# Two 2 MB stores taken out of SyncE's stream and issued as 64 GpSimd pieces and 4 SyncE pieces

## The chip, the cores and the metric

The kernel runs on one core of a Trainium2 chip. The metric is the time of one execution on the device in microseconds. Before the change the median of three runs is 730.11 us (729.95 to 731.11).

## The reference

One decode step of a transformer block, forward and backward. `x` is one token of width 640; the caches hold 32 heads of 8192 rows of 128 values, bf16; `d...` below are the gradients that the kernel must return as well.

```python
xn  = layernorm(x)
q   = (xn @ wq) as 32 heads of 128
p_h = softmax(k_cache_h @ q_h / sqrt(128))        # 8192 values per head
o_h = p_h @ v_cache_h
out = x + concat(o_h) @ wo + (silu(xn @ w1) * (xn @ w3)) @ w2
# backward from grad_out: dx, dk_cache, dv_cache, dwq, dwo, dw1, dw3, dw2
# dv_cache_h = outer(p_h, do_h)       dk_cache_h = outer(ds_h, q_h)
```

Each head reads a K and a V of 2 MB and writes a dK and a dV of 2 MB. That is nearly all of the traffic: 151 MB read and 151 MB written.

## The kernel before, in words

A K or V of one head is one tile `kv` of 128 partitions with 8192 values each (16 KB per partition); ten such slots exist. `head(h)` runs for h = 0 to 31: TensorE transposes the K and V tiles and multiplies them with q and do, ScalarE evicts, VectorE makes the softmax. One head later, VectorE overwrites the same tiles with the outer products (L466, two halves for V, two for K): `outers_a(h-1)` makes dV and calls `store("V", h-1)`, `outers_b(h-1)` finishes dK and calls `store("K", h-1)`. So V28, V29, V30 and V31 below are the tiles whose dV is stored, K28 to K31 those whose dK is stored.

What orders the work around the change:

- **SyncE's queue.** All K and V loads and stores go through `fifo` (L105) on SyncE, in program order: a store, then the next load as soon as slots allow. Each is one transfer of 128 rows of 16 KB. At the end stands this order: load K31, store K27, load V31, then store V28, K28, V29, K29, V30, K30, V31, K31, then a part of the last `wo` and `wq` gradients, then the two small output rows (L849, L867). SyncE issues in order, so a store that isn't ready holds back all that stand behind it. V31's load is the last load.
- **GpSimd's queue.** GpSimd carries the weight groups: one store of `wo_g` (640 KB, L507) and five of `wq_g` (128 KB each, L527) per group of four heads. In heads 29 to 31 these are the `wo_g` store of group 6 and its five `wq_g` stores. At the very end `store_group` (L505 to L511) splits the `wo_g` and `wq_g` stores of the last group by partitions: 0 to 67 by SyncE, 68 to 72 and 73 to 127 by GpSimd.
- **Eight semaphores per kind of queue.** Transfers of SyncE take eight completion semaphores in turn, those of GpSimd another eight. A transfer that takes a semaphore again waits until the transfer eight before it on that kind of queue has landed.

The lines that the change touches:

```python
    def store(kind, h):
        t = kv_tiles.pop((kind, h))
        if kind == "K":
            hd.pop(h)
        fifo((dkc if kind == "K" else dvc)[h], t[:])
        free_slots.append(t)
        load_next()
```

Of the kernel before, what the change touches and what calls it, by code (L numbers as in the profile page):

```python
# [21 lines left out]
def kernel(  # L22
# [22 lines left out]
    nc = tc.nc  # L45
    H = A_k_cache.shape[1]
# [10 lines left out]
    KVN = J * DH  # L57
# [18 lines left out]
    dkc = out_2.rearrange("b h (p j) d -> (b h) p (j d)", p=P)  # L76
    dvc = out_3.rearrange("b h (p j) d -> (b h) p (j d)", p=P)
# [26 lines left out]
    def fifo(out_, in_):  # L104
        nc.sync.dma_start(out_, in_)  # L105
# [16 lines left out]
    def load_next():  # L122
        if not pending or len(free_slots) < lag[0]:
            return
        kind, h = pending.pop(0)
        t = free_slots.pop(0)
        fifo(t[:], (kc if kind == "K" else vc)[h])
        kv_tiles[(kind, h)] = t
# [335 lines left out]
    def outer(dst, vec, pair, lo, hi):  # L464
        n = hi - lo
        nc.vector.tensor_tensor(  # L466
            dst[:, lo * DH:hi * DH].rearrange("p (j a b) -> p j a b", a=DH // 2, b=2),
            vec.rearrange("p (a b) -> p a b", b=2).unsqueeze(1).to_broadcast([P, n, DH // 2, 2]),
            pair[:, lo:hi, :].unsqueeze(2).to_broadcast([P, n, DH // 2, 2]), ALU.mult)
# [4 lines left out]
    def outer_k(h, lo, hi):  # L474
        outer(kv_tiles[("K", h)], hd[h]["qd"][:, 0, :], hd[h]["U2"], lo, hi)

    def store(kind, h):
        t = kv_tiles.pop((kind, h))
        if kind == "K":
            hd.pop(h)  # L480
        fifo((dkc if kind == "K" else dvc)[h], t[:])
        free_slots.append(t)
        load_next()

# [248 lines left out]
    def outers_a(h):  # L733
        outer_v(h, 0, J // 2)
        outer_v(h, J // 2, J)
        store("V", h)
        outer_k(h, 0, J // 2)

    def outers_b(h):
        outer_k(h, J // 2, J)  # L740
        store("K", h)
# [156 lines left out]
```

## Time and profile before

| what | value |
|---|---|
| median of three runs | 730.11 us |
| the profiled execution | 730.34 us, of which the span on the core is 728.6 us |
| TensorE, VectorE, ScalarE, GpSimd busy | 84%, 63%, 52%, 6% of the span |
| DMA, mean over the span | 417 GB/s, 303.52 MB |
| SyncE's queue (q1 in the profile) | 277.09 MB |
| GpSimd's queue (q0 in the profile) | 25.61 MB |
| last load (V31) issued, landed | 659.79 us, 685.38 us |
| last outer product done, its store issued | 704.85 us, 704.87 us |
| last output row issued | 716.75 us |

Times inside the execution are counted from the start of the span. The profile page has the busy share of each engine, the share of the 16 DMA engines in 40 slices, and the DMA queues with packets and bytes. Other views of the trace list who waited for whom, the busy time in chosen stretches, and the DMA packets in a stretch. The trace also records each DMA packet with its start, its duration, its size and its queue (but not the engine that moved it), and each increment of a completion semaphore by a DMA engine; for a transfer of 128 rows there are 16 of these, one for each DMA engine. From these come the times at which the first and the last engine finished a transfer.

### The profile page before, as it was taken

How to read it: one execution, taken by the hardware profiler on the slowest of the kernel's cores; microseconds unless marked ns; L12 is line 12 of the kernel's file. 1: busy time of each engine (PE TensorE's matmuls, PEld its weight loads, DVE VectorE, ACT ScalarE, POOL GpSimd, SP SyncE). 2: the span in 40 equal slices, each digit the busy share in tenths (PEclk: the TensorE clock that was granted, in tenths of full speed). 3: DMA queues.
4: the chain of work that ended last, by engine and by line, in shares of the span. 5: the costliest groups of instructions: out<-in, count | busy, mean ns of one | idle time of the engine just before them, and what ended most of it. 6: DMA issues, size and time to landing. Idle time of an engine off the chain costs nothing.

```text
span 728.6 us, 12970 instructions
## 1 busy us (share of the span) xinstructions
PE 608.4 (84%) x5193; PEld 378.6 (52%) x5193; DVE 459.7 (63%) x811; ACT 376.6 (52%) x727; POOL 44.1 (6%) x75
## 2 busy tenths in 40 slices
PE   4989489999899989878897997978898889979840
PEld 2547366655565556544564554544555556545520
DVE  4169646688868776666466665646746657576482
ACT  3640736665666566554464554645555446555510
POOL 0010100010001000101000000001000000000000
PEclk9996799999999999998898998999999989998965
DMA  9999999999999999999999999999999999999994
GB/s 355 399 411 419 432 425 430 426 426 422 419 426 429 428 423 427 426 429 425 427 428 426 430 421 430 429 428 429 424 427 430 426 430 429 426 430 427 430 402 157
DMA packets 28186, 303.52 MB, mean 417 GB/s; under 512 B 3379, under 2 KB 5355, under 8 KB 11486
## 3 DMA queue, kind: packets, MB, share of 16 engines
q1 hardware_dynamic: 21962, 277.09, 89.8%
q0 software_dynamic: 6160, 25.61, 8.8%
q8 instruction: 41, 0.67, 0.4%
q14 instruction: 19, 0.16, 0.1%
q10 hardware_dynamic: 4, 0.00, 0.0%
HBM read 151.34 MB, written 151.34 MB: 415 GB/s over the span
## 4 chain that ended last, share of the span: by engine, by line
DMA 49%; PE 37%; DVE 7%; ACT 4%; issue 1%; SPq 0%; ACTq 0%; DVEq 0%
DMA out_dram<-kv 21%; PE pT L318 17%; DMA kv<-in_A_k_cache_dram 15%; DMA kv<-in_A_v_cache_dram 11%; PE sA L339 5%; PE dA L339 4%; PE X L433 4%; DVE kv L466 3%; PE m L356 2%; DMA wo_g<-in_A_wo_dram 2%; ACT KT L320 1%; ACT kv L642 1%; PE gu_ps L561 1%; DVE side L257 1%; PE dh_ps L572 1%
## 5 line engine op out<-in xcount | busy, mean ns | idle before, releaser
L320 ACT COPY KT<-pT 128x512 f32<-128x512 f32 x512 | 288.5, 588 | 229.3 <-PE pT L318 210.4
L318 PE MATMUL pT<-ident_f,kv 128*128 128x128 f32 x2048 | 307.9, 289 | 54.5 <-DMA kv<-in_A_k_cache_dram 40.7
L318 PEld LDWEIGHTS pT<-ident_f,kv 128*128 128x128 f32 x2048 | 236.8, 149 | 146.1 <-PE pT L318 51.9
L466 DVE TENSOR_TENSOR kv<-qd,U 128x4096 bf16<-128x4096 bf16 x64 | 146.1, 2285 | 0.0
L466 DVE TENSOR_TENSOR kv<-qd,P 128x4096 bf16<-128x4096 bf16 x64 | 143.6, 2285 | 0.0
L433 PE MATMUL X<-kv,Z 128*32 128x512 bf16 x1024 | 102.0, 431 | 1.8 <-DVE Z L450 1.8
L339 PE MATMUL dA<-KT,qz 128*32 128x512 bf16 x512 | 85.4, 413 | 0.0
L339 PE MATMUL sA<-KT,qz 128*32 128x512 bf16 x512 | 82.5, 402 | 0.0
L416 DVE SCALAR_TENSOR_TENSOR U<-m,P 128x64 bf16<-128x64 f32 x32 | 7.5, 233 | 105.7 <-PE m L356 105.7
L433 PEld LDWEIGHTS <-Z 128*32 128x32 bf16 x1024 | 33.9, 104 | 38.1 <-issue 13.2
L339 PEld LDWEIGHTS <-qz 128*32 128x32 bf16 x1024 | 29.5, 95 | 41.0 <-issue 38.5
L382 DVE TENSOR_REDUCE mrow<-m 128x1 f32<-128x64 f32 x32 | 7.2, 224 | 51.6 <-PE m L356 51.4
L356 PEld LDWEIGHTS m<-selc,KT 64*128 64x128 f32 x256 | 22.0, 147 | 31.8 <-ACT KT L346 18.0
L356 PE MATMUL m<-selc,KT 64*128 64x64 f32 x256 | 31.1, 246 | 8.0 <-ACT KT L346 8.0
L527 POOL DMA_DIRECT2D out_dram<-wq_g x35 | 19.1, 547 | 223.1 <-DVE wq_g L524 124.3
L376 ACT CAST qd<-pT 128x256 bf16<-128x256 f32 x32 | 11.9, 373 | 38.8 <-DVE kv L466 30.4
L389 DVE TENSOR_REDUCE negM<-m 128x1 f32<-128x128 f32 x32 | 9.3, 292 | 32.8 <-PE m L386 32.8
L522 DVE SCALAR_TENSOR_TENSOR wq_g<-wq_g,side 128x512 bf16<-128x512 bf16 x40 | 27.3, 683 | 0.0
L257 DVE SCALAR_TENSOR_TENSOR side<-wo_g,g_bc 128x640 bf16<-128x640 bf16 x32 | 26.3, 820 | 0.6 <-DMA wo_g<-in_A_wo_dram 0.2
L507 POOL DMA_DIRECT2D out_dram<-wo_g x7 | 5.3, 761 | 282.5 <-DVE qz L363 240.3
L448 DVE SCALAR_TENSOR_TENSOR U<-m,P 128x128 bf16<-128x128 f32 x32 | 11.4, 356 | 16.8 <-PE m L446 16.8
L346 ACT COPY KT<-dA 64x512 f32<-64x512 f32 x32 | 18.6, 582 | 5.1 <-PE dA L339 5.0
(163 smaller groups left out, 386.0 us busy)
## 6 DMA issues: line engine op xcount, KB each, us to landing
out_dram<-kv SPq DMA_DIRECT2D x64, 2048.0 KB, 30.7
kv<-in_A_k_cache_dram SPq DMA_DIRECT2D x32, 2048.0 KB, 17.2
kv<-in_A_v_cache_dram SPq DMA_DIRECT2D x32, 2048.0 KB
wq_g<-in_A_wq_dram POOLq DMA_DIRECT2D x7, 640.0 KB, 13.6
wo_g<-in_A_wo_dram POOLq DMA_DIRECT2D x7, 640.0 KB, 19.4
out_dram<-wo_g POOLq DMA_DIRECT2D x7, 640.0 KB, 11.3
out_dram<-wq_g POOLq DMA_DIRECT2D x35, 128.0 KB, 6.8
kv<-in_B_w_dram SPq DMA_DIRECT2D x2, 1728.0 KB
```

The source lines that it names most:

```text
L257: nc.vector.scalar_tensor_tensor(junk[:], G_["wo"][:, hh, :], 1.0, g_bc[:], ALU.mult, ALU.mult, accum_out=G_["do"][:, hh:hh + 1])
L318: nc.tensor.transpose(pT[:, k * P:(k + 1) * P], W3[:, 4 * c + k, :], ident_f[:])
L320: nc.scalar.copy(KT[:].rearrange("p k w -> p (k w)"), pT[:])
L339: nc.tensor.matmul(S_[kind][q:q + QW, :], lhsT=S_["qz"][:, o:o + QW], rhs=KTb[c][:, par, :], start=(c0 == 0 and par == 0), stop=(c0 == NCH ...
L346: nc.scalar.copy(XS[0:QH].rearrange("p k w -> p (k w)"), S_.pop(kind)[0:QH, :])
L356: nc.tensor.matmul(S_["m"][:, b0:b0 + 4 * J].rearrange("p (x c k t) -> p k x c t", x=4, k=4, t=2)[:, k], lhsT=XS[0:QH, k, :], rhs=selc[0:Q ...
L376: nc.scalar.copy(qd[:].rearrange("p a d -> p (a d)"), hd[h].pop("ps_r"))
L433: nc.tensor.matmul(xg["X"][q:q + QW, :], lhsT=Z[:, o:o + QW], rhs=W[:, N4 * i:N4 * (i + 1)], start=(slot == 0 and i < 4), stop=(slot == NS ...
L448: nc.vector.scalar_tensor_tensor(S_["U2"][:], S_["V"][:, 0:J].unsqueeze(2).to_broadcast([P, J, 2]), S_["m"][:, OC + NS:OC + NS + 1], S_["P ...
L466: nc.vector.tensor_tensor(dst[:, lo * DH:hi * DH].rearrange("p (j a b) -> p j a b", a=DH // 2, b=2), vec.rearrange("p (a b) -> p a b", b=2 ...
L522: nc.vector.scalar_tensor_tensor(wq_g[:, ci, :], wq_g[:, ci, :], 1.0, dqb, ALU.mult, ALU.mult, accum_out=dxa[:, ci, g:g + 1])
L527: nc.gpsimd.dma_start(dwq_g[:, ci, :], wq_g[:, ci, :])
```

## The change

The dV stores of heads 28 and 29 (`CUT_V`) no longer go through `fifo`. Each is cut into 34 transfers. GpSimd issues 32 of them: four rounds for each half of the partitions `s`, each with four rows, one row, three rows and eight rows, every fourth partition. The one row is only the last 61 values (122 bytes) of a partition of 16 to 19 or 48 to 51. The first 8131 values of these eight partitions go out on SyncE in two transfers of four rows.

```diff
+    CUT_V = (H - 4, H - 3)
+    CT = KVN - 61
+
+    def store_cut(dst, t):
+        def rows(eng, r0, n, step, c0=0, c1=KVN):
+            sl = slice(r0, r0 + (n - 1) * step + 1, step)
+            eng.dma_start(dst[sl, c0:c1], t[sl, c0:c1])
+
+        for s in (0, 32):
+            for b in range(4):
+                rows(nc.gpsimd, s + b, 4, 4)
+                rows(nc.gpsimd, s + 16 + b, 1, 1, CT, KVN)
+                rows(nc.gpsimd, s + 20 + b, 3, 4)
+                rows(nc.gpsimd, 64 + s + b, 8, 4)
+            rows(nc.sync, s + 16, 4, 1, 0, CT)
+
     def store(kind, h):
         t = kv_tiles.pop((kind, h))
         if kind == "K":
             hd.pop(h)
-        fifo((dkc if kind == "K" else dvc)[h], t[:])
+        dst = (dkc if kind == "K" else dvc)[h]
+        if kind == "V" and h in CUT_V:
+            store_cut(dst, t)
+        else:
+            fifo(dst, t[:])
         free_slots.append(t)
         load_next()
```

In GpSimd's program the order becomes: `wo_g` store of group 6, 32 pieces of V28, three `wq_g` stores, 32 pieces of V29, two `wq_g` stores, and the four last stores of group 7. In SyncE's program the two stores become two transfers each, in the same places. Nothing else moves on any engine.

## The prediction

> **What bounds the kernel now.** I read the end first, by stretches: the last three columns are clock, share of the 16 DMA engines, GB/s.
>
> ```profile
> 700.00:712.00 12.00, 1.81 (x12) 0.88 (x12) 10.72 (x23) 0.59 (x1) 1.32 (x2) 0.50 0.98 409
> 712.00:718.00 6.00, 0.93 (x3) 0.59 (x3) 2.29 (x12) 0.00 (x0) 1.33 (x2) 0.50 0.81 288
> ...
> 720.00:722.00 2.00, 0.00 (x0) 0.00 (x0) 0.00 (x0) 0.00 (x0) 0.00 (x0) 0.50 0.17 63
> 722.00:727.00 5.00, 0.00 (x0) 0.00 (x0) 0.00 (x0) 0.00 (x0) 0.00 (x0) 0.50 0.06 26
> ```
>
> No engine computes after 718, and from 722 to 727 the DMA share is 0.06 = 1/16: one DMA engine alone is still at work. Next, what SyncE waits for from 700 on (total, times, longest):
>
> ```profile
> SPq L893 <- DMA out_dram<-kv: 5.7, 2, 4.9
> ...
> SPq L893 <- DMA out_dram<-fin_bf: 3.6, 1, 3.6
> ```
>
> The output rows have landed at 722.3; then SyncE waits 4.9 us more, for a 2 MB store. The landing records of that store (K31, issued 704.87) show 15 engines done between 711.65 and 718.44 and the last at 727.35; the span ends 1.2 us later. The same engine was last everywhere: on V31's load the slowest of the others finished at 677.61, it at 685.38. Call it the **laggard**. It gates V31's load, the start of the last compute chain (685.4 to 715.8), and the end.
>
> Then the packets of 722.2 to 726.9, and GpSimd's rows of the page:
>
> ```profile
> DMA packets 11, 0.11 MB, mean 24 GB/s; under 512 B 4, under 2 KB 4, under 8 KB 4
> ...
> q1 hardware_dynamic: 7, 0.11, 5.7%
> q0 software_dynamic: 4, 0.00, 0.1%
> ```
>
> ```profile
> L527 POOL DMA_DIRECT2D out_dram<-wq_g x35 | 19.1, 547 | 223.1 <-DVE wq_g L524 124.3
> ...
> out_dram<-wo_g POOLq DMA_DIRECT2D x7, 640.0 KB, 11.3
> out_dram<-wq_g POOLq DMA_DIRECT2D x35, 128.0 KB, 6.8
> ```
>
> On the laggard, SyncE's 16 KB packets (0.611 us each in the packet records) alternate with tiny GpSimd packets. The full engines show the rule: of the `wq_g` store issued at 646.17, one engine's data packets start at 649.87 and 650.63 and its semaphore packet at 651.40, each with one SyncE packet between. So **while an engine has SyncE work, each GpSimd packet waits for one SyncE packet**. And a GpSimd transfer of few rows puts packets on engines that carry none of its rows: after the 5-row store of 707.68 an engine shows 16 bytes at 712.36 and the 4-byte semaphore at 712.98, a SyncE packet between. The four last GpSimd stores leave 77 packets of 16 bytes and 80 of 4 bytes behind.
>
> **What goes away.** Partitions 16 to 19 and 48 to 51 are 8 of 128 rows, one engine's share. Is it the laggard's? SyncE's 68-row stores run on four engines (four late landings, 716.4 to 717.3, when the laggard had two 2 MB stores to go), so it is none of those. In the last 55-row GpSimd store it shows 16-byte packets at 720.84, 721.45 and on, so it carries none of its rows either; 11 engines carry those, five the 5-row store. It is the fifth of that group, which these partitions fit if the groups start where the change counts them from. Its queue loses 2 × 8 × 0.611 = **9.8 us**, all behind V31's load, so K31's store ends on it at 727.35 − 9.8 ≈ 717. Then others are last: the four engines of the 68-row stores, with the output rows at 722.3. Had the pieces cost nothing, the span would end at 722.4 + 1.2 = 723.6: **−4.9 us**.
>
> **What is added on SyncE.** Four transfers replace two: 0.46 us of issue each at most, while SyncE waits anyway. The second V29 piece reuses the semaphore of the store issued at 637.81, which landed at 669.85: it leaves at 669.9, not 665.5, and K29 waits for K31's load (675.2, now 674.61). Engines have work queued then (K29 landed 31 us after issue), so 0. The four engines get 4 × 0.61 = 2.4 us more; they idle 2.7 us now, from V30's end at 693.15 to 695.85 (K30 issued 694.59, and 8 packets before its landing at 700.72), so 0; without that gap +2.4.
>
> **What is added on GpSimd.** 64 pieces, in order, ahead of five `wq_g` stores and the last four stores. Issue costs 0.55 to 0.6 each (543 ns for 128 rows, 590 for five). But a piece waits for the landing of the piece eight before, on all 16 engines, and each engine gives it two turns: data or 16 bytes, then the semaphore. On an engine with SyncE work a turn costs one 0.611 us packet, and its own row another 0.611, once in four pieces. So four pieces take 8 × 0.611 + 0.611 = 5.5 us, **1.38 us a piece**, and eight in flight cover the 4 us from issue to first packet. Bounds: below, the pace of issue, 0.6; above, three turns for every piece, 1.85. I take 1.38, from the rows with both packets. By the Trainium skill, DMA: Bandwidth & Descriptors, section Anatomy of one DMA — SWDGE (gpsimd) path, a transfer takes 2.0 us plus its bytes at 436 GB/s: an estimate of 2.15 us for 64 KB, eight at once, hence the pace of issue and the fast rival below. The trace's 6.8 us for 128 KB, where that gives 2.3, speaks against it under load.
>
> Now the clock:
> 1. V28 is ready at 642.7 (outer product 638.19 + 4.49). Issue 643.0, first packets 3.7 later (as 646.17 to 649.87) at 647. 32 × 1.38 = 44.2: done at 691.
> 2. Three `wq_g` stores, queued behind: each three turns and 2 × 0.16, 2.1; 6.4 in all: 697.5.
> 3. V29 (ready 665.5) starts only now. The slower of the other engines have SyncE work until about 713.5: 718.1 now, less 5 rows of V29 not yet served (3.1), less 2.2 of late small stores, plus 0.6 of tiny packets. (713.5 − 697.5)/1.38 = 11.6 pieces done, eight more issued.
> 4. From 713.9 GpSimd issues the other 12.4 at 0.6: 7.4; two `wq_g` 1.1; four last stores 0.59 + 0.73 + 0.58 + 0.77 = 2.7: last issue over at 725.1. Now it is at 714.0.
> 5. To landing: 1.1 to 2.9 to the first packet (as for the stores of 712.66 and 707.68), 25 KB per engine 1.0, landing 0.4: about 728.3. GpSimd's drain ends 1.0 later (now 725.9, its last landing 724.91), the final barrier takes 0.7: **730.0**.
>
> Against 728.6 that is **+1.4**; I say +1.5 and, on the median, 730.11 + 1.5 = **731.6 us**. (The profiled execution took 730.34 with a span of 728.6, the difference stays.)
>
> What hides the rest: V31's load is not delayed. The laggard gains about 60 tiny packets (0.6 us) and loses three `wq_g` stores (1.0) ahead of it; the others carry some 6 rows of V28 (3.5 us) and end at 681.1, under 685.4. That cover is 7.8 us; both heads' rows together, 9.8, would pass it by 2, straight into the compute chain. No load waits for V28's or V29's slot, and nothing reads the `wq_g` of group 6 again, so GpSimd's delay shows only at the end.
>
> **The rivals.**
> - *Pieces at the pace of issue* (0.6 each): V28 done by 667, V29 by 690, the last stores on time; the gain of 4.9 stays: 725.2 us. For: GpSimd has nothing else to do, and the stores of `wq_g` show 543 ns. Against: the alternation of packets. The point of decision is 1.3 us a piece; below it the kernel gets faster.
> - *Three turns for each piece*, 1.85, or GpSimd slowed by VectorE in its issue: by 713.5 only about 32 pieces are through, 23.5 are left to issue, the end comes 6.5 us later: 738. For: the slowest of 16 engines sets each landing. Against: eight pieces in flight even out which engine carries a row.
> - *The laggard is not the engine relieved.* It ends at 727 as now, hidden under the pieces' tail: 730 to 732. For: which engine takes which partition is in no record. Against: the groups above. The Trainium skill, same page, section Latency and other measured facts, has engines 7 and 15 usually slower, by which these partitions would be the wrong ones; the 16-byte packets on the laggard speak for the fifth engine here.
> - *The pieces' tail just meets the end*: 1.25 to 1.35 a piece, within 1.4 us of now.
>
> **How the numbers follow.** What a measurement of this kernel can tell from no change is about 0.2%, 1.5 us. Tail of pieces sets the end, as summed: 0.45 (own range 729.5 to 735). Tail meets the end: 0.15. Pace of issue: 0.22. Three turns: 0.1. Wrong engine: 0.08. Range 725.0 to 737.0: it takes in the fast rival and most of the slow one. My sum sits on the edge of 0.2%, so its case splits: slower 0.46 (0.3 of the first, 0.1, 0.06), same 0.30 (0.15, 0.13, 0.02), faster 0.24 (0.22 and 0.02).
>
> **What would show it.** Right: GpSimd's pieces of V28 spread over some 40 us, V29's starting near 690 and still issuing after 713, last GpSimd issue near 725, and the last wait not for `out_dram<-kv` from SyncE's laggard. Wrong: pieces 0.6 apart, last `wo_g` issue at 707.7 as now. V31's load landing after 686 would break the claim that it is covered; SyncE stores of K31 still landing at 727 would name the wrong engine.

## The result, and the profile after

The changed kernel takes 754.75 us (median of four runs, 752.66 to 757.23), the kernel before 730.57 us beside it (729.95 to 731.11): a ratio of 1.033, 95% interval 1.030 to 1.037. The profiled execution took 754.99 us with a span of 753.2. The prediction was 731.6 us, so some 23 us are to be explained.

The busy time by stretches of the changed kernel, with clock, DMA share and GB/s at the end of each line:

```profile
700.00:712.00 12.00, 8.45 (x75) 5.10 (x73) 9.44 (x12) 3.95 (x9) 4.50 (x9) 0.83 0.66 257
712.00:718.00 6.00, 1.81 (x12) 0.88 (x12) 4.88 (x9) 0.59 (x1) 2.02 (x4) 0.50 1.03 391
718.00:724.00 6.00, 0.15 (x1) 0.18 (x2) 5.49 (x21) 0.00 (x0) 1.99 (x4) 0.50 0.89 341
724.00:730.00 6.00, 0.78 (x3) 0.41 (x3) 1.12 (x5) 0.00 (x0) 1.52 (x4) 0.50 0.36 141
730.00:736.00 6.00, 0.00 (x0) 0.00 (x0) 0.00 (x0) 0.00 (x0) 1.59 (x4) 0.50 0.27 88
736.00:742.00 6.00, 0.00 (x0) 0.00 (x0) 0.00 (x0) 0.00 (x0) 3.85 (x7) 0.50 0.38 125
742.00:748.00 6.00, 0.00 (x0) 0.00 (x0) 0.00 (x0) 0.00 (x0) 1.33 (x2) 0.50 0.46 140
```

Two things differ from before. At 700 to 712 TensorE still has 8.45 us of work (1.81 before) and the DMA engines are two thirds busy: the last compute chain runs late. And from 724 to 742, where nothing is left but stores, the DMA share is 0.27 to 0.38: on average four to six of sixteen engines work.

**The late chain.** The first transposes on V31's tile, in TensorE's timeline, before and after (start, length, and in brackets the idle time ahead and who ended it):

```profile
685.52 1.06 PE L318 MATMUL pT<-ident_f,kv 128*128 128x128 f32 x8 [1.49 <-DMA kv<-in_A_v_cache_dram]
```

```profile
694.45 1.94 PE L318 MATMUL pT<-ident_f,kv 128*128 128x128 f32 x8 [4.30 <-DMA kv<-in_A_v_cache_dram]
```

V31's load comes 8.9 us later. Fifteen engines have delivered it by 683.82, one at 694.32. The chain behind it ends 10.45 us later: K31's store goes out at 715.32 (704.87 before).

**The late end.** SyncE's timeline after (start, length of the issuing instructions):

```profile
717.86 0.29 SPq L105 DMA_DIRECT2D out_dram<-wo_g  x1
722.88 0.29 SPq L105 DMA_DIRECT2D out_dram<-wq_g  x1
723.59 14.80 SPq L869 DMA_DIRECT2D out_dram<-KT  x2
738.48 5.11 SPq L887 DMA_DIRECT2D out_dram<-fin_bf  x2
```

and before:

```profile
713.10 2.49 SPq L849 DMA_DIRECT2D out_dram<-KT  x2
715.77 2.10 SPq L867 DMA_DIRECT2D out_dram<-fin_bf  x2
```

The two output rows from `KT` took 2.49 us to issue; now they take 14.80. SyncE does not wait for a semaphore in that time: the issuing instructions themselves are long. GpSimd's own waits between 640 and 753 (total, times, longest), and its last pieces and stores in its timeline:

```profile
POOL out_dram L483 <- DMA out_dram<-kv: 52.4, 45, 3.1
```

```profile
735.42 1.98 POOL L483 DMA_DIRECT2D out_dram<-kv  x4 [3.08 <-DMA out_dram<-kv]
737.88 1.13 POOL L547 DMA_DIRECT2D out_dram<-wq_g  x2 [0.48 <-DMA out_dram<-kv]
740.53 1.32 POOL L531 DMA_DIRECT2D out_dram<-wo_g  x2 [1.52 <-DMA out_dram<-kv]
742.46 1.33 POOL L531 DMA_DIRECT2D out_dram<-wq_g  x2 [0.61 <-DMA out_dram<-kv]
```

45 of the 64 pieces wait for an earlier piece to land. The issues themselves are cheap, as the page's group shows (64 of 507 ns):

```profile
L483 POOL DMA_DIRECT2D out_dram<-kv x64 | 32.3, 507 | 65.5 <-DMA out_dram<-kv 52.4
```

V28's pieces go from 642.39 to 685.01, V29's from 691.33 to 736.90 (the starts of the first and the last), and the last store leaves GpSimd at 743.8 (714.0 before). The kernel ends on GpSimd: its last store lands at 748.49, its closing drain ends at 752.10. SyncE's last landing is at 748.84.

**Where the rows went.** The trace's packets name no engine, but packets that follow one another without a gap can be strung into sixteen chains. (Where two packets begin together a link can be wrong, so the counts can be off by one.) From 645 to 666, in V28's pieces, one chain has data of every piece (10 rows and three 122-byte packets), two have 9 or 10 rows, one 7, four have 4, and eight have none. Those are the counts for pieces of 4, 1, 3 and 8 rows if each begins at the *same* engine: per head 24 rows on the first three engines, 16 on the fourth, 8 on the next four, none on the other eight. The end shows it too: the four pieces issued from 735.42 to 736.9 have 15 rows of 16 KB, one for each of 15 engines had they followed one another, 0.6 us of work. Together with the rows still queued they run one behind another until 743.2.

The theory that follows is that a piece of n rows always lands on the first n engines. The laggard, if it is the fifth, so gets eight rows of V28 ahead of V31's load, and the first four get a pile of rows that holds back everything at the end. Rivals: 64 transfers are too many as such (turns); uneven transfers slow all packets; GpSimd's rows overtake the load whatever their form.

### The profile page after: what moved, and what is told of

Same layout as the page of the kernel before. It is cut to its first block, busy times and chain, and to the rows that moved or that the text cites. A ratio compares the mean times of both kernels' runs of the same rounds, so it can differ in the third digit from the quotient of the medians.

```text
span 753.2 us, 13039 instructions
## 1 busy us (share of the span) xinstructions
PE 606.7 (81%) x5193; PEld 378.7 (50%) x5193; DVE 459.9 (61%) x811; ACT 377.3 (50%) x727; POOL 76.5 (10%) x139
## 4 chain that ended last, share of the span: by engine, by line
DMA 56%; PE 32%; DVE 4%; ACT 3%; issue 2%; POOL 1%; SPq 0%; POOLq 0%; ACTq 0%; DVEq 0%
DMA out_dram<-kv 29%; DMA kv<-in_A_k_cache_dram 19%; PE pT L318 15%; DMA kv<-in_A_v_cache_dram 7%; PE sA L339 4%; PE X L433 3%; PE dA L339 3%; DVE kv L466 2%; PE m L356 2%; DMA wo_g<-in_A_wo_dram 1%; ACT KT L320 1%; ACT kv L662 1%; PE gu_ps L581 1%; PE dh_ps L592 1%; PE dx_acc L680 1%
## 5 line engine op out<-in xcount | busy, mean ns | idle before, releaser
L433 PE MATMUL X<-kv,Z 128*32 128x512 bf16 x1024 | 96.6, 414 | 1.8 <-DVE Z L450 1.8
L339 PE MATMUL sA<-KT,qz 128*32 128x512 bf16 x512 | 84.3, 409 | 0.0
L483 POOL DMA_DIRECT2D out_dram<-kv x64 | 32.3, 507 | 65.5 <-DMA out_dram<-kv 52.4
L356 PEld LDWEIGHTS m<-selc,KT 64*128 64x128 f32 x256 | 21.6, 144 | 29.1 <-ACT KT L346 18.7
L448 DVE SCALAR_TENSOR_TENSOR U<-m,P 128x128 bf16<-128x128 f32 x32 | 11.4, 356 | 15.5 <-PE m L446 15.5
```

The source lines that it names most:

```text
L339: nc.tensor.matmul(S_[kind][q:q + QW, :], lhsT=S_["qz"][:, o:o + QW], rhs=KTb[c][:, par, :], start=(c0 == 0 and par == 0), stop=(c0 == NCH ...
L356: nc.tensor.matmul(S_["m"][:, b0:b0 + 4 * J].rearrange("p (x c k t) -> p k x c t", x=4, k=4, t=2)[:, k], lhsT=XS[0:QH, k, :], rhs=selc[0:Q ...
L433: nc.tensor.matmul(xg["X"][q:q + QW, :], lhsT=Z[:, o:o + QW], rhs=W[:, N4 * i:N4 * (i + 1)], start=(slot == 0 and i < 4), stop=(slot == NS ...
L448: nc.vector.scalar_tensor_tensor(S_["U2"][:], S_["V"][:, 0:J].unsqueeze(2).to_broadcast([P, J, 2]), S_["m"][:, OC + NS:OC + NS + 1], S_["P ...
L483: eng.dma_start(dst[sl, c0:c1], t[sl, c0:c1])
```

## The experiments

All are compared with the kernel before on the same chip (730.5 to 731.2 us there).

### 1. Both heads as one GpSimd transfer each

```diff
-        if kind == "V" and h in CUT_V:
-            store_cut(dst, t)
+        if kind == "V" and h in (H - 4, H - 3):
+            nc.gpsimd.dma_start(dst, t[:])
```

> V28 and V29 each leave as one GpSimd transfer of 128 rows, nothing is cut. Theory P (piling: a GpSimd transfer of fewer than 16 shares always starts on the same first engine, so the rows of the cut stores pile up on three engines, 24 of 16 KB each per head): with 128 rows every engine carries its own 8 rows, so nothing piles, V31's load lands within 1 us of 685 and the time is that of before, 728 to 733 us. Rival T (turns: 64 pieces with two turns each are the whole loss, where the rows go doesn't matter): the same here, since there are two transfers and not 64. Rival G (a 2 MB store on GpSimd's queue runs beside SyncE's stream instead of in it and starves the loads): V31's load late by 5 us or more, 735 us or more. The run tells G from the other two.

Measured: 734.99 us, ratio 1.007 (1.005 to 1.008). GpSimd's timeline shows that it is held by nothing (V28, V29), and V31's tile is late all the same:

```profile
640.92 0.54 POOL L483 DMA_DIRECT2D out_dram<-kv  x1 [7.62 <-DVE kv L466]
...
670.27 0.54 POOL L483 DMA_DIRECT2D out_dram<-kv  x1 [14.49 <-DVE kv L466]
```

```profile
694.99 1.07 PE L318 MATMUL pT<-ident_f,kv 128*128 128x128 f32 x8 [0.49 <-DMA kv<-in_A_v_cache_dram]
```

That is rival G's late load, with a time at the edge of its range. Sixteen rows on every engine (2 × 8) are 16 × 0.611 = 9.8 us, and the load is 9.5 us late: rows that GpSimd issues share the engine with the loads that SyncE has queued, where SyncE's stores would have stood behind V31's. So the delay of the load needs no small pieces. Moving the two stores to GpSimd costs 4.5 of the 24 us; the rest comes with cutting them.

### 2. Sixteen neighbouring rows to a piece

```diff
-            store_cut(dst, t)
+            for r in range(0, P, 16):
+                nc.gpsimd.dma_start(dst[r:r + 16], t[r:r + 16])
```

> V28 and V29 each leave as eight GpSimd transfers of 16 neighbouring rows; one row for each engine, no rows on SyncE. Theory P: no piling, 8 rows per engine and head, so V31's load is not late by more than 2 us and the time is 728 to 735 us. Rival T: 16 pieces with two turns and a row each take 16 x 1.83 = 29 us in all instead of 88, so most of the loss goes as well; between 730 and 736 us. Rival M (rows read by an engine other than the one that owns their partitions collide with the owner's packets and double their time): packets of 16 KB that take 0.9 to 1.2 us appear as they did in the changed kernel, and the time stays above 738 us.

Measured: 743.21 us, ratio 1.018 (1.015 to 1.020). Strung into chains as above, from 643 to 660, every engine has 5 to 8 of the rows, so nothing is piled up. Instead the packets get long: of those issued from 640 to 700, 154 of 1,252 take over 0.8 us, up to 3.6, where 0.611 is the rule (5 of 1,486 before, all beside an instruction fetch). They sum to 140 us above 0.611, 8.8 per engine, and V31's load lands at 701.5. A second way to lose, then, with pieces that are spread evenly. Rival M forecast long packets and such a time; that its cause is the right one is not shown.

### 3. SyncE alone, 120 and 8 rows

```diff
-            store_cut(dst, t)
+            fifo(dst[0:120], t[0:120])
+            fifo(dst[120:P], t[120:P])
```

> V28 and V29 each leave on SyncE as 120 rows and 8 rows, nothing on GpSimd. If 120 rows go to the first 15 engines, 8 each, and 8 rows to the first 8, one each, the sixteenth engine is freed of 2 x 8 x 0.611 = 9.8 us. Theory P says that GpSimd's 55-row store of before starts on the first engine too and covers engines 1 to 11, so that the laggard, which carried none of it, is one of the last five. If it is the sixteenth, K31's last landing comes some 9 us earlier and the time falls by 3 to 5 us, to 725 to 728 us. If it is another of the last five, it is 0 to 2 us, either way. My own prediction's reading (the laggard is the fifth engine): no gain, 730 to 732 us.

Measured: 741.74 us, ratio 1.015 (1.013 to 1.017). None of the expected times came. There is no GpSimd piece at all, V31's load is 1.3 us late (686.65), and yet there are 208 packets over 0.8 us after 664, and SyncE's last `wq_g` store takes 11.0 us to issue. The long packets and the held SyncE are thus not GpSimd's own.

### 4. V28 alone, and 5. V29 alone

```diff
-    CUT_V = (H - 4, H - 3)
+    CUT_V = (H - 4,)        # experiment 4
+    CUT_V = (H - 3,)        # experiment 5
```

> The changed kernel with V28 alone cut. Theory P: the piling of V28 alone (24 rows on the first three engines before V31's load) makes that load late by about 9 us on one engine, so the compute chain and the last stores are late by 7 to 10 us, and the time is 736 to 742 us, though GpSimd has finished V28's pieces by 690 and has nothing left at the end. Rival T: the loss is the tail of V29's pieces; without them GpSimd's last stores are on time and the time is 726 to 731 us.

> Only V29 is cut (32 GpSimd pieces, SyncE's two transfers of four rows); V28 is stored by SyncE as before. Theory 1 (in the changed kernel two delays add up: V28's rows and tiny packets stand ahead of V31's load on the engine that is last, +8 us, and V29's pieces keep GpSimd busy into the end because they start after V28's): here V29's pieces start at about 666 and last to about 712, V31's load lands at 687 to 690 instead of 694, the last GpSimd issue is at 716 to 722, the time 730 to 736. Theory 2 (each cut store costs its 10 to 12 us wherever it stands, since cutting V28 alone gave +10): 738 to 742. Theory 3 (only V28's rows ahead of the load count, the tail is nothing by itself): within 1.5 of before, 729 to 732, with K31's store on its last engine earlier than 727.

Measured: V28 alone 740.18 us, ratio 1.013 (1.012 to 1.014); V29 alone 740.55, ratio 1.013 (1.011 to 1.015). Each costs 9 to 10, both 24. But each in its own way. With V28 alone V31's load is as late as in the changed kernel (first line below); with V29 alone it is 2.7 us late (second line, another kernel), and SyncE is held for long at the end (third):

```profile
693.71 1.94 PE L318 MATMUL pT<-ident_f,kv 128*128 128x128 f32 x8 [4.10 <-DMA kv<-in_A_v_cache_dram]
```

```profile
688.20 1.06 PE L318 MATMUL pT<-ident_f,kv 128*128 128x128 f32 x8 [0.80 <-DMA kv<-in_A_v_cache_dram]
```

```profile
715.11 11.37 SPq L105 DMA_DIRECT2D out_dram<-wq_g  x1
726.57 2.76 SPq L869 DMA_DIRECT2D out_dram<-KT  x2
```

For V29 alone the time is in theory 2's range. The mechanism of theory 1 came as expected up to the last GpSimd issue (over at 716.7), but not its end. There K31's store lands on its last engine at 729.10, and the two 68-row stores behind it at 733.38 and 736.98: the four engines of these stores are the last ones. None of the three theories had that. (The 11.4 us of SyncE's issue are over at 726.5, before those engines come to the store.)

### 6. A probe: four transfers at the end

Parts of K30, V31 and K31 are kept back and issued by GpSimd as its last transfers; the remainders go out by SyncE.

```diff
+    for i in (1, 2, 3, 0):        # 68, 17, 51 and 104 rows
+        nc.gpsimd.dma_start(*probes[i])
```

> The kernel before, except that parts of three late stores are kept back and issued by GpSimd at the very end, one behind the other, when the DMA engines are idle: transfers of 68, 17, 51 and 104 rows of 16 KB, which run on 4, 1, 3 and 8 engines if a transfer takes the largest divisor of its rows up to 16. 4 + 1 + 3 + 8 = 16, as the pieces of 4, 1, 3 and 8 rows in the change. If each transfer begins at the engine behind the last one's (what the prediction took for granted), no engine has more than 17 of these rows: 17 x 0.611 = 10.4 us, all landed some 15 us after the first issue, and the last stretch shows nearly all engines busy. If each begins at the same engine, that one has 17 + 17 + 17 + 13 = 64 rows: 39 us, and the DMA share falls step by step to 1/16. The time itself (before plus 10 to 45 us) is not the point.

Measured: the DMA share is 0.76 to 1.05 up to 732 and 0.47 to 736, the last landing of the four at 740.2, 25 us after the first issue. Neither came: the rows are not on 4, 1, 3 and 8 engines.

```profile
724.00:726.00 2.00, 0.00 (x0) 0.00 (x0) 0.00 (x0) 0.00 (x0) 0.00 (x0) 0.50 0.76 209
...
732.00:734.00 2.00, 0.00 (x0) 0.00 (x0) 0.00 (x0) 0.00 (x0) 0.00 (x0) 0.50 0.48 177
...
736.00:738.00 2.00, 0.00 (x0) 0.00 (x0) 0.00 (x0) 0.00 (x0) 0.00 (x0) 0.50 0.30 98
```

The landings of the first three engines to finish say how the rows are dealt out:

```
68 rows:  718.80 718.93 721.73, the others 722.61 to 728.67
17 rows:  718.96 719.10 721.90
51 rows:  719.14 719.27 722.06
104 rows: 719.43 724.34 726.63
```

One engine has nothing of all four, a second nothing of the first three, a third a little of the first and nothing of the next two. That is the pattern of n/16 rows, rounded up, to each engine from the first one on until they are used up: 68 rows are 5 each on 13 engines and 3 on the 14th; 51 are 4 on 12 and 3 on the 13th; 104 are 7 on 14 and 6 on the 15th. No transfer begins where the last one ended. With n up to 16 the same rule gives one row to each of the first n engines, as the chains showed.

By the Trainium skill, DMA: Bandwidth & Descriptors, section Why a DMA increments its semaphore by 16 and not by 1, a GpSimd transfer on fewer than 16 engines takes consecutive ones from a round-robin cursor, except that some direct copies get the partitions over 16, rounded up, on each engine. The pieces and this probe follow the exception. The packets fit: the changed kernel has 77 packets of 16 bytes from 640 on, as many as the kernel before, so the pieces put none, only data and the 4-byte semaphores. The 5-row and 55-row stores at the end of the kernel before seem to follow the cursor: in their stretch the four engines of SyncE's 68-row stores, and the laggard, show only the 16-byte packets of the 55-row store. No run here shows what decides between the two.

### 7. Without the 122-byte pieces

```diff
-    CT = KVN - 61
+    CT = KVN
-                rows(nc.gpsimd, s + 16 + b, 1, 1, CT, KVN)
```

> The changed kernel without its 122-byte pieces: SyncE's four-row transfers carry the whole 16 KB, GpSimd has 24 pieces a head instead of 32. If the rows of the pieces all begin at the same engine (theory 1), the rows stay piled as they are and only the turns of 16 tiny transfers go: the pieces of V28 end near 677 to 681 (now 685), V31's load lands at 692 to 694 (now 694.3), the last GpSimd issue comes 14 to 20 us earlier than 743.8, the end is set by the compute chain and the piled stores: 738 to 745. If the turns of small transfers were all of the loss (theory 2), a quarter of the loss goes at V31's load as well: load at 691, and 748. If the packets of 16,262 bytes are what slows others (theory 3), packets over 0.8 us are gone here apart from those beside an instruction fetch.

Measured: 750.83 us, ratio 1.026 (1.025 to 1.028). A quarter of the pieces is gone and 4 us are saved, so the time is above both theories'. V31's load still lands at 693.92: its delay is not made of tiny turns. The last GpSimd issue ends at 735.5, 8.3 us earlier and less than the 14 to 20 expected, because the pieces become slower: 1.66 us each after the first eight, 1.57 with the tiny ones between. Packets over 0.8 us are no fewer (111 after 664, 98 in the changed kernel), so the 16,262-byte packets are not what causes them.

### 8. Four-row pieces only

V28 alone; each eight-row piece becomes two of four rows.

```diff
-                rows(nc.gpsimd, 64 + s + b, 8, 4)
+                rows(nc.gpsimd, 64 + s + b, 4, 4)
+                rows(nc.gpsimd, 80 + s + b, 4, 4)
```

> V28 alone is cut (740.2 us, V31's load at 693.6), and its eight-row pieces are issued as two four-row pieces each, so that the head has 40 pieces. If every piece begins at the same engine, four-row pieces stay on the first four, and the engine that is last (the fifth) carries none of V28's rows: 8 x 0.611 = 4.9 us less ahead of V31's load, which lands at 688 to 690 although there are more pieces; the time falls by 4 to 5 to 735 to 737. If pieces follow one another round all engines, eight more pieces only mean more turns: V31's load at 694 to 695, the time 740 to 742.

Measured: 743.85 us, ratio 1.017 (1.015 to 1.019). The load first:

```profile
685.70 1.06 PE L318 MATMUL pT<-ident_f,kv 128*128 128x128 f32 x8 [0.22 <-DMA kv<-in_A_v_cache_dram]
```

With eight more pieces than experiment 4, the load lands at 685.56 instead of 693.57, within 0.2 us of the kernel before. So the laggard is one of engines five to eight, which eight-row pieces reach and four-row pieces do not; in the kernel before, the engines without rows of the 55-row store are the first four and the laggard, which leaves the fifth if they are neighbours. V28's eight rows on it were thus the delay of the load: 8.0 us, where eight packets of 0.611 are 4.9. What the other 3.1 us are is not shown; some packets over 0.8 us and, in experiment 4 alone, packets of the `wq_g` stores stood ahead of the load as well. But the time did not fall, it rose:

```profile
718.00:724.00 6.00, 0.00 (x0) 0.00 (x0) 0.00 (x0) 0.00 (x0) 0.00 (x0) 0.50 0.32 133
724.00:730.00 6.00, 0.00 (x0) 0.00 (x0) 0.00 (x0) 0.00 (x0) 0.00 (x0) 0.50 0.23 79
730.00:736.00 6.00, 0.00 (x0) 0.00 (x0) 0.00 (x0) 0.00 (x0) 0.00 (x0) 0.50 0.24 78
```

```profile
712.68 17.58 SPq L105 DMA_DIRECT2D out_dram<-wq_g  x1
730.35 3.06 SPq L870 DMA_DIRECT2D out_dram<-KT  x2
733.50 2.45 SPq L888 DMA_DIRECT2D out_dram<-fin_bf  x2
```

A DMA share of 0.24 is four engines of sixteen. They carry all of V28 (34 rows on each of the first three, 26 on the fourth, with SyncE's two four-row pieces), and SyncE's 68-row store, which runs on four engines too, takes 17.58 us to issue. My expected 735 to 737 counted the load and forgot the pile.

### 9. The same, with the last stores on 16 engines

```diff
-        fifo(dst[0:68], t[0:68])
-        for lo, hi in ((68, 73), (73, P)):
+        fifo(dst[0:64], t[0:64])
+        for lo, hi in ((64, P),):
```

> As the run in which V28 alone leaves in four-row pieces (743.9 us; there the issue of SyncE's 68-row wq_g store took 17.6 us and the output rows left at 730 to 735.6), but SyncE's part of the last wo_g and wq_g stores is 64 rows (16 engines, 4 rows each) and GpSimd's is the other 64. If SyncE was held because the four engines with the pieces had no room for more, the issue of the wq_g store takes under 2 us here, the output rows leave before 725, V31's load stays at 685 to 687, and the end is set by what the four engines still have to do: 733 to 739. If SyncE was held by something else (GpSimd's pieces as such, a semaphore), the issue takes 10 us or more again and the time stays at 742 to 745.

Measured: 738.16 us, ratio 1.010 (1.008 to 1.011), in the range of the first theory.

```profile
712.56 0.59 SPq L105 DMA_DIRECT2D out_dram<-wq_g  x1
713.26 2.28 SPq L870 DMA_DIRECT2D out_dram<-KT  x2
715.93 4.88 SPq L888 DMA_DIRECT2D out_dram<-fin_bf  x2
```

```profile
718.00:724.00 6.00, 0.00 (x0) 0.00 (x0) 0.00 (x0) 0.00 (x0) 0.00 (x0) 0.50 0.54 170
724.00:730.00 6.00, 0.00 (x0) 0.00 (x0) 0.00 (x0) 0.00 (x0) 0.00 (x0) 0.50 0.29 107
```

The same store now takes 0.59 us to issue and the output rows leave at 713 to 720.8 instead of 730 to 736. So 17 rows for each of the piled engines hold SyncE, and four rows for each do not. What is left is those engines' own work, until 735.

But the 5.7 us that the time falls are not SyncE's wait. The last landing of K31's store is the same in both runs, 733.59 in experiment 8 and 733.37 here. Behind it, the `wo_g` and `wq_g` stores of SyncE land last at 737.17 and 740.77 in experiment 8, 3.58 and 3.60 us for 17 rows on one engine, and at 734.21 and 735.06 here, 0.84 and 0.85 us for four rows. (Seventeen rows are 87 KB, 3.2 us at 16 KB in 0.611.) The difference is 5.5 us. The long issue was over at 730.3, before that engine had K31's store behind it, so it cost nothing by itself: the fullest engine sets the end.

### 10. The control for it: the split at 64 alone

The same edit of `store_group` in the kernel before.

> The control: the kernel before with nothing but the split of the last wo_g and wq_g stores at 64 rows instead of 68, 5 and 55. The engine that is last gets 8 rows of each, 8 x (5,120 + 5,120 bytes) = 82 KB, where it now has the share of the 5-row stores, one row; at 16,384 bytes in 0.611 us that is some 2.7 us more for it. Theory 1 (the fullest engine sets the end): 731 to 734. If the split itself were what made the run with four-row pieces faster by 5.7 us, this would be faster than the kernel before: 725 to 728.

Measured: 732.83 us, ratio 1.003 (1.002 to 1.005). The split by itself costs 2 us where there is no pile; it helps only where the engines of the 68-row stores are the fullest. The last landing moves from 727.35 (K31's store) to 730.55 (SyncE's `wq_g` store): 3.2 us, where 2.7 were worked out for the rows that the laggard gets.

### 11. Half of V28 in four-row pieces

```diff
-        for s in (0, 32):
-            for b in range(4):
-                rows(nc.gpsimd, s + b, 4, 4)
...
+        for r in range(0, 64, 16):
+            for b in range(4):
+                rows(nc.gpsimd, r + b, 4, 4)
+        fifo(dst[64:P], t[64:P])
```

> As the run before it (V28 in four-row pieces, the last wo_g and wq_g stores split 64 and 64; 738.2 us), but only rows 0 to 63 of V28 leave in GpSimd pieces (16 pieces of four rows); rows 64 to 127 go out by SyncE as one 64-row transfer, four rows on each engine. The first four engines lose 12 of their rows against that run (7.3 us), the engine that is last in the kernel before has 4 rows less than there (2.4 us). Theory 1 (the rows on the fullest engine set the end): 729 to 732, V31's load at 685 to 686, the output rows on time. Theory 2 (what costs is that packets slow one another as soon as transfers are uneven): 735 to 739, with tens of packets over 0.8 us.

Measured: 734.36 us, ratio 1.005 (1.004 to 1.006), between the two theories. With half of the pieces the end comes 3.8 us earlier than in experiment 9, where the 12 rows less of the expectation were worth 7.3. V31's load lands at 687.83, 2.5 us later than there, with two more engines at 687.34 and 684.87, so the laggard is no longer alone. There are 76 packets over 0.8 us after 664 (12 in the control); what they cost is not separated. It does not beat the kernel before.

### 12. The laggard relieved ahead of the load

In the kernel before, K27's store is issued as 68 and 60 rows.

```diff
+        if (kind, h) == ("K", H - 5):
+            fifo(dst[0:68], t[0:68])
+            fifo(dst[68:P], t[68:P])
```

> The kernel before with one edit: the store of K27, which stands directly ahead of V31's load on SyncE, is issued as 68 and 60 rows. If a transfer begins at the same engine and uses the largest divisor of its rows up to 16, the 68 rows go to the first four engines (17 each), the 60 to fifteen (4 each): the engine that is last (the fifth) loses 4 rows, 2.4 us, ahead of V31's load, and the first four, 17 us ahead of it there, get 13 rows more, 7.9 us. Theory 1 (only the rows of the last engine count for the load): V31's load lands at 683 (now 685.4), K31's store goes out at 702.5, and the end then depends on the first four engines, which also carry the 68-row stores of the last weights: 728 to 734. Theory 2 (uneven transfers slow all packets, as the 120-row stores did): packets over 0.8 us in numbers from 665 on, V31's load not earlier, 736 to 742.

Measured: 742.51 us, ratio 1.015 (1.014 to 1.017). V31's load lands at 688.72, 3.3 us later:

```profile
688.85 1.94 PE L318 MATMUL pT<-ident_f,kv 128*128 128x128 f32 x8 [4.71 <-DMA kv<-in_A_v_cache_dram]
```

Twelve engines have finished it by 682.40, and the four others end at 683.18, 683.79, 688.20 and 688.72. Theory 1 was wrong in a size: I had taken the first four engines to be the five that finish this load at 668 before. Two of them have less than 8 us to spare, 13 rows more made them the last. Theory 2 had its long packets too (67 from 640 to 700), so both count, and this run does not separate them.

## Why the prediction was wrong

- **The step that failed** is "its own row once in four pieces", in the pieces' pace, and with it "the laggard gains about 60 tiny packets (0.6 us)". I took pieces of 4, 1, 3 and 8 rows to follow one another round the sixteen engines. They all begin at the first. From that come the larger errors below.
- **"V31's load is not delayed"**: it landed at 694.32, and the prediction had named a landing after 686 as what would break the claim. The laggard got eight rows, not eight 122-byte packets; experiment 8 takes them away and the delay is gone. They cost 8.0 us where 8 × 0.611 is 4.9. The cover of 7.8 us that I had worked out was the other engines' distance to the laggard; it says nothing of rows on the laggard itself.
- **Relief of 9.8 us on the laggard**: never seen, since it got back by the eight-row pieces as many rows as were taken from it. That it is the fifth engine fits, and is not shown: experiments 4 and 8 leave the fifth to the eighth.
- **1.38 us a piece**: the mean over V28's 32 pieces is 42.6 / 31 = 1.37, and that is chance. The first eight need not wait and leave 0.5 apart; after them it is 1.57, with whole rows alone 1.66 and 1.69 (experiments 7 and 11). My rival of three turns, 1.85, counted the turns of the first engine rightly, which has a row of its own in every piece, but not for this reason. And "two turns" on every engine was wrong: an engine without a row of a piece gets the 4-byte semaphore alone.
- **"The slower engines end 713.5, then 0.6 a piece"**: V29's pieces stayed at 1.4 to 1.5 until 735. They wait for the engines that the pieces themselves have filled. The last GpSimd issue was over at 743.8, not 725.1: +18.7 of the 23 us. (The late compute chain alone holds it only to 724.8, as experiment 4 shows, where the load is as late.) From there to the end it took 9.4 us, not 4.9; 2.6 of the difference are GpSimd's drain, which ended 3.6 us behind its last landing and not 1.0.
- **"What is added on SyncE", taken as 0**: its four-row pieces land on the engines with the pile, and its last stores queue there. The 68-row `wq_g` store landed last at 748.67 (722.13 before). SyncE's issue was held for 14.8 and 5.1 us besides (2.5 and 2.1 before); by experiment 9 that is a sign of the pile and not a cost of its own.
- The sign of the change was in the likeliest case, the range was not wide enough, and no rival had this mechanism: they took the spreading for granted and argued about turns, or about which engine is relieved.

The extra 24 us are so two losses of about 10, one for each head (experiments 4 and 5): eight rows of V28 ahead of the last load, and a pile on the first engines that holds the last stores. No run has V28's late load without a pile, so how its 9.7 us divide is open.

Cutting both costs 5 us more than the sum (24.2 against 9.7 and 9.4). About 3 of these are GpSimd's drain: it holds the final barrier until 752.1, where SyncE is done at 749.4. Its lag behind GpSimd's last landing goes with the number of GpSimd transfers in the kernel: 1.00 us with 67 (before), 1.65 with 83 (experiment 2), 2.30 with 99 (4 and 5), 2.63 with 107 (8), 2.95 with 115 (7) and 3.61 with 131 (the changed kernel), which is 0.04 us for each. Why is not shown. The prediction left it at 1.0.

**What stays open:** why packets of 16 KB take up to 3.6 us in some arrangements. It came with neighbouring rows in pieces (2), with 120, 68 and 60 rows (3, 12) and with strided pieces after about 664 (98 of them from 664 to 745 in the changed kernel, 62 us in all, 3.8 per engine), and not with whole tiles (1) nor in the first 20 us of the strided pieces. Which partition an engine reads at that moment is in no record, so I did not settle it.

## What to carry to other kernels

Before cutting a store to balance the DMA engines, find out on which engines small transfers land: here every GpSimd piece began at the same first engine, and SyncE's 68-row stores ran on the same four that the pieces had filled, so many pieces were a pile and not a spread. An engine that is behind decides when a load lands, and a store from another queue gets in ahead of a load that is already queued; count rows on that one engine, ahead of that one load. A DMA share of 0.25 at the end is four engines of sixteen, and says so before any theory.

## What the hardware showed unexpectedly

- **SyncE's issue can be held for long.** The instruction that issues a 68-row store took 0.27 us before, 11.37 and 17.58 us in experiments 5 and 8, and 0.59 us with 64 rows (9). It did not set the end in these runs: the engines that it waited for did.
- **TensorE's clock after a wait.** Eight transposes took 1.94 us behind waits of 4.10, 4.30 and 4.71 us (experiment 4, the changed kernel, experiment 12) and 1.06 behind waits of 0.22 to 2.79 us (2.79 in experiment 7), all ahead of V31's tile. The granted clock after the wait, in the changed kernel:

```profile
694.00:696.00 2.00, 1.55 (x8) 1.57 (x8) 0.00 (x0) 0.37 (x1) 0.43 (x2) 0.59 0.97 389
696.00:698.00 2.00, 2.00 (x10) 0.84 (x9) 0.00 (x0) 1.34 (x3) 0.66 (x2) 0.55 0.57 223
698.00:700.00 2.00, 2.00 (x19) 1.32 (x18) 0.23 (x1) 1.21 (x3) 0.64 (x2) 1.00 0.31 127
```

  It is 0.59 and 0.55 for some 4 us and then 1.00; before the change it is 1.00 throughout that stretch. So a load that is 8.9 us late made the chain 10.45 us late. By the Trainium skill, TensorE: Matmul & The Clock Gate, section Part 1: The HAM clock gate (the "warmup" mystery), the clock halves after an idle window of about 3.4 us and comes back after a busy one as long. The slow stretch of some 4 us agrees. The idle time does not quite: ahead of earlier tiles, eight transposes took 1.94 us behind a wait of 2.42 us (experiment 4, at 679.54) and 1.06 behind one of 2.89 us (experiment 12, at 675.44), so the length of the wait alone does not decide.
